# HGRN2 scan and hierarchical MoE on one core: the last two chunks routed as one, two more units halved, kept rows sent in pieces

## The chip, the cores and the metric

The kernel runs on one core of a Trainium2 chip. TensorE (PE in the profile, its weight loads PEld) multiplies; VectorE (DVE), ScalarE (ACT) and GpSimd (POOL) do element-wise work; SyncE (SP) issues most transfers, GpSimd the gathers, scatters and some small ones, ScalarE a few. The metric is the device time of one execution in microseconds (us). Before the change it is 399.38 us, the median of three runs (397.52 to 401.21).

## The reference

Inputs are q, k, v and f_logit of 4 batches x 8 heads x 768 steps x 48 (fp32), and the weights of a mixture of 4 groups x 4 experts, each 384 -> 1024 -> 384. First comes a gated linear recurrence for each head:

```python
f = 1.0 / (1.0 + np.exp(-f_logit))
for t in range(S):
    state = f[:, :, t, :, None] * state + np.einsum('bhd,bhe->bhde', k[:, :, t], v[:, :, t])
    y[:, :, t] = np.einsum('bhd,bhde->bhe', q[:, :, t], state)
```

y, with the heads side by side, gives 3072 rows x of 384 numbers. Each row goes to one expert (the best group, then the best expert of that group), and its result is scaled by both softmax weights:

```python
g_idx = np.argmax(x @ w_group, axis=1)
e_idx = np.argmax(xg @ w_expert[g], axis=1)
out[tok_idx] = combined[:, None] * (np.maximum(xg[mask_e] @ w1[g, e], 0.0) @ w2[g, e])
```

## The kernel before, in words

**Two stages.** The first stage works the recurrence off in 6 chunks of 128 steps, each in two units of two batches (`units`, NU = 12 units, numbered 0 to 11; unit i belongs to chunk i // 2). The second stage passes over the 16 experts, the fullest first ("places" 0 to 15 of a ranking), with rows gathered from a DRAM copy of x, `x_dram`. All four engines TensorE, VectorE, ScalarE and SyncE run in an order written out by hand; a wait is only for data or for a buffer.

**The written order.** For each i a list of tokens (`EVEN`, `ODD`, and `ORDERS` for i = 8 to 12) says which step of which unit comes next; `step` runs one. A token is a letter and an offset to i. `l` issues loads, `c` clamps the gate logits on VectorE, `g` makes decays on ScalarE with sums on TensorE, `m` multiplies q and k by them on VectorE, `t` transposes on TensorE, `z` copies halves of v on ScalarE, `s` makes scores (`scored`: matmuls, then a mask product on VectorE), `n` updates the states, `w` sums the outputs (`weighed`: a state part and a value part), `d` makes router logits (`done`), `x` turns the rows (`listed`), `b` transposes decays. `r` advances the routing, `e` the first two experts, `o` sends kept rows, `1` to `4` ask for the weights of the first two experts (first layers, then second layers). An engine works its own part of the list in this sequence, so what stands ahead of a step on the same engine delays it.

**Halved units.** For units in `HALVED` (3 to 8) `scored` leaves out the quarter of the score matrix that lies above the diagonal, and masks 384 instead of 512 columns; `weighed` takes 64-row pieces in the value part, and needs the v halves copied by `z`. The other units go through `scored_whole`.

**Routing.** `route` is a generator for one chunk (4 batches): best group and expert (VectorE, in two steps), ranks within the experts (`rk`, TensorE), running counts, the slots (`ln`, `head`, `val`, VectorE), the scales (written to x_dram with GpSimd, `meta`), and a table of row numbers (`tb` on TensorE, added to `table` on VectorE). With chunk 3 (CLOSE) the two fullest experts so far are named, their first 128 rows are gathered (`early`), and `fix_early` notes them in the counts; it runs inside the routing of chunk 4 as `tidy`. After the last chunk `chosen` gathers the second 128 rows of place 1 (`rows_w`), ranks all experts (`ranked`) and finds all row numbers and names (`choose`).

**Hand-over.** `early` runs under the tokens `e`: a transposing step for each of the two experts, four `up` steps each (six matmuls of 128 columns, 12 instructions, then a ReLU), and the first five of eight `down` matmuls of expert 0. Then the list ends. Next come, in program order, the transposes of the gathered second rows of place 1 (`turn_in`), the last three down matmuls, and the second half of place 1's first layer. From there on PSUM banks come from `bank` with `turns` set: it zeroes banks on VectorE as they are first taken, three with the first request, which is that of the transposes.

**Kept rows.** Rows of units 0 to 7 stay in two buffers (of the pool for second-layer weights) and go to x_dram with two transfers of 1536 KB on SyncE, at the token `o`; rows of units 8 to 11 are sent one by one by GpSimd or ScalarE (`side`).

Of the kernel before, what the change touches and what calls it, by code (L numbers as in the profile page):

```python
# [23 lines left out]
def kernel(  # L24
# [128 lines left out]
    firsts = iota([P, B * (G + 1), 4], [[0, B * (G + 1)], [-1, 4]], "firsts", base=4)  # L153
# [37 lines left out]
    limits = const([1, (ARMS - 1) * GE + 80], FP32, "limits")[:, 0:(ARMS - 1) * GE].rearrange("p (a e) -> p a e", e=GE)  # L191
# [18 lines left out]
    def route(c, lg, sb, tabled=True, tidy=None, counted=None, last=None):  # L210


        def tmp(shape, name, dtype=FP32, bufs=1):
            return sb.tile(shape, dtype, tag=name, bufs=bufs, name=name)

        SHP = (P, B * (G + 1), 4)
        L = lg.rearrange("p n (a e) -> p (n a) e", e=4)
        mx = tmp([P, B * (G + 1)], "mx")
# [4 lines left out]
        nc.vector.scalar_tensor_tensor(out=oh, in0=dl, scalar=0.0, in1=firsts, op0=OP.is_ge, op1=OP.mult)  # L223
        yield
        best = tmp([P, B * (G + 1)], "best")
        nc.vector.reduce_max(out=best, in_=oh, axis=AX)
        nc.vector.tensor_tensor(oh, oh, best.unsqueeze(2).broadcast_to(SHP), OP.is_equal)
        ohv = oh.rearrange("p (n a) e -> p n a e", n=B)
        ohe = tmp([P, B, GE], "ohe", BF16)
        nc.vector.tensor_tensor(ohe.rearrange("p n (g e) -> p n g e", e=EG), ohv[:, :, 1:G + 1, :],  # L230
                                ohv[:, :, 0, :].unsqueeze(3).broadcast_to((P, B, G, EG)), OP.mult)
        yield

        rk = bank([P, B + 1, GE], "rk")
        nc.tensor.matmul(rk[:, 0:B, :].rearrange("p n e -> p (n e)"), lhsT=strictb, rhs=ohe.rearrange("p n e -> p (n e)"), start=True, stop=False, skip_group_check=True)
        for n in range(B):
            nc.tensor.matmul(rk[:, n + 1:, :], lhsT=onesb, rhs=ohe[:, n:n + 1, :].broadcast_to((P, B - n, GE)), start=False, stop=(n == B - 1), skip_group_check=True)
        nc.scalar.activation(dl, dl, AF.Exp)
        yield
        if tidy:  # L240
            tidy(sb)
        pick = tmp([P, B, GE], "pick")
        nc.vector.tensor_tensor(pick, rk[:, 0:B, :], run.unsqueeze(1).broadcast_to((P, B, GE)), OP.add)
        nc.vector.tensor_tensor(pick, pick, ohe, OP.mult)
        nc.vector.reduce_sum(out=keys[:, c], in_=pick, axis=AX)
        nc.vector.tensor_tensor(run, run, rk[:, B, :], OP.add)
        if counted:
            counted(sb)
        yield
        ln = val = None  # L250

        def slots():

            nonlocal ln, val
            at = tmp([P, B, 2], "at", I32)
            nc.vector.tensor_copy(at[:, :, 0], keys[:, c])
            nc.vector.tensor_scalar(at[:, :, 1], at[:, :, 0], 7, None, OP.logical_shift_right)
            nc.vector.tensor_scalar(at[:, :, 0], at[:, :, 0], P - 1, None, OP.bitwise_and)
            atf = tmp([P, B, 2], "atf")
            nc.vector.tensor_copy(atf, at)  # L260
            ln = tmp([P, B, P], "ln", BF16)
            nc.vector.tensor_tensor(ln, lanes.unsqueeze(1).broadcast_to((P, B, P)), atf[:, :, 0:1].broadcast_to((P, B, P)), OP.is_equal)
            yield
            BLK = (P, B, 2 * GE)
            head = tmp(list(BLK), "head")
            nc.vector.tensor_tensor(head, heads_of.rearrange("p e j -> p (e j)").unsqueeze(1).broadcast_to(BLK), atf[:, :, 1:2].broadcast_to(BLK), OP.is_equal)
            val = tmp([P, 2, B, 2 * GE], "val", BF16)
            for m in range(2):
                nc.vector.tensor_tensor(val[:, m], head, part[:, c, :, m:m + 1].broadcast_to(BLK), OP.mult)
            yield  # L270

        def scales():

            sm = tmp([P, B, G + 1], "sm")
# [3 lines left out]
            ew = tmp([P, B, G], "ew")  # L278
            nc.vector.tensor_tensor(ew, sm[:, :, 1:G + 1], ohv[:, :, 0, :], OP.mult)
            ws = tmp([P, B], "ws")  # L280
            nc.vector.reduce_sum(out=ws, in_=ew, axis=AX)
            meta = tmp([P, B, 2], "meta", bufs=2)
            nc.vector.tensor_tensor(meta[:, :, 0], ws, sm[:, :, 0], OP.mult)
            nc.gpsimd.tensor_copy(meta[:, :, 1].bitcast(I32), token[:, c, :])
            nc.gpsimd.dma_start(out=rows_of(c)[:, :, DM:RW], in_=meta)
            yield

        for part_of in (scales, slots) if last else (slots, scales):
            if tabled or part_of is scales:
                yield from part_of()  # L290
        if tabled:
            tb = bank([P, 2, GE, 2], "tb")
            for b in range(B):
                nc.tensor.matmul(tb.rearrange("p m e j -> p m (e j)"), lhsT=ln[:, b], rhs=val[:, :, b, :], start=(b == 0), stop=(b == B - 1))
# [191 lines left out]

    def room(w, shape, name):

        own_size = {"bufs": 1} if w["pool"] is ep and name == "h" else {}
        full = w["pool"].tile([P, shape, P if w["pool"] is ep else WIDE], FP32, tag=name, name=name, **own_size)  # L490
        w[name[:2].replace("xe", "xT") + "_full"] = full
        return full[:, :, 0:w["n"]]
# [116 lines left out]
    def early():  # L609
# [6 lines left out]
        full = ep.tile([P, FO, WIDE], FP32, tag="h_full", bufs=1, name="h_full")  # L616
        ws[WHOLE].update(h=full[:, :, 0:P], h_full=full)
        nc.gpsimd.tensor_copy(told, ws[0]["x"][:, 0, DM:RW])
# [9 lines left out]
    with ExitStack() as fast:  # L628
# [36 lines left out]
        HALVED = range(3, NU - 3)  # L665
# [166 lines left out]
        def weighed(i):  # L832
# [13 lines left out]
            for asked in (E, L) if i in HALVED else ():  # L846
                for a in range(HP):
# [11 lines left out]
        def done(i):  # L859
# [3 lines left out]
            if s == 0:  # L863
                groups[c] = sb.tile([P, B, NL], FP32, tag="lgs", name="lgs")
            lT = bank([P, P], "lT")
            for a in range(HP):
                for b in range(2):
                    at = 32 * (2 * b + a % 2)
                    nc.tensor.matmul(lT[at:at + 32, :], lhsT=gw[:, b, a, :], rhs=xT[:, b, a, :], start=(a < 2), stop=(a >= 2), skip_group_check=True, tile_position=(0, at))
# [5 lines left out]
            nc.vector.reduce_sum(out=groups[c][:, 2 * s:2 * s + 2, :], in_=lg[:, :, :, 0:NL].rearrange("p b j l -> p b l j"), axis=AX)  # L875
            if s:
                routes.append(routed(c))
# [43 lines left out]
        def routed(c):  # L921

            yield from route(c, groups[c], sb, tidy=fix_early if c == CLOSE + 1 else None, counted=load_early if c == CLOSE else None,
                             last=chosen if c == NC - 1 else None)
# [13 lines left out]
        def advance(gens):  # L938
# [24 lines left out]
        def step(nm, i):  # L963
# [6 lines left out]
            elif nm == "o":  # L970
                send_kept(i - (NU - 4))
# [266 lines left out]
```

## Time and profile before

| what | us |
|---|---|
| median of three runs | 399.38 |
| lowest and highest | 397.52, 401.21 |
| the profiled execution | 398.24 |
| its span, first to last instruction | 396.4 |
| TensorE busy in the span | 388.4 (98%) |
| VectorE busy | 285.8 (72%) |
| ScalarE busy | 164.4 (41%) |
| GpSimd busy | 90.3 (23%) |

Matmuls are pipelined and their ends are modelled, so the busy time of TensorE tells where it had work and not how fast it did it. A chain of waits goes back from the last instruction to what released each step; a run of TensorE pieces in it means that nothing else held the kernel there. The granted clock of TensorE is 0.997 of full speed (2.4 GHz) over the span.

### The profile page before, as it was taken

What the parts mean: (1) busy time and instruction counts of PE and PEld (TensorE: products, weight loads), DVE (VectorE), ACT (ScalarE), POOL (GpSimd) and SP (SyncE); (2) the same over time, 40 slices, a digit from 0 to 9 for tenths busy, and PEclk for the clock granted to TensorE, in tenths of its full rate; (3) what the DMA queues carried; (4) which work ended last, traced back from release to release, by engine and by line L of the source; (5) the groups of instructions that cost most, each with busy time, mean ns of one, the idle gap of its engine ahead of it and who ended that gap; (6) DMA issues with size and microseconds to landing.
All of it is one profiled execution on the core that took longest, in us unless ns stands there. A gap on an engine that the chain in (4) does not pass through costs nothing.

```text
span 396.4 us, 10685 instructions
## 1 busy us (share of the span) xinstructions
PE 388.4 (98%) x4150; PEld 361.7 (91%) x4150; DVE 285.8 (72%) x845; ACT 164.4 (41%) x368; POOL 90.3 (23%) x171
## 2 busy tenths in 40 slices
PE   8999999999999999999999999999999999999994
PEld 3888888888888979999999999999999999999992
DVE  6766788878998687970999949578687585596530
ACT  6777888888665311222312223123131232232130
POOL 7000010101031157102042222321320430110241
PEclk9999999999999999999999999999999999999998
DMA  9999989799969849994938659578587596585110
GB/s 188 216 200 204 199 169 183 145 186 258 258 207 382 310 145 330 387 389 187 318 100 316 212 193 347 157 279 267 175 330 236 180 361 201 194 333 170 34 50 28
DMA packets 133038, 89.44 MB, mean 226 GB/s; under 512 B 103441, under 2 KB 123619, under 8 KB 132955
## 3 DMA queue, kind: packets, MB, share of 16 engines
q1 hardware_dynamic: 125666, 75.50, 63.8%
q0 software_dynamic: 6656, 11.93, 9.5%
q8 instruction: 62, 1.02, 1.0%
q10 hardware_dynamic: 632, 0.83, 0.6%
q14 instruction: 22, 0.17, 0.1%
HBM read 78.71 MB, written 9.89 MB: 223 GB/s over the span
## 4 chain that ended last, share of the span: by engine, by line
PE 73%; issue 15%; DMA 4%; POOL 3%; DVE 2%; POOLq 1%; ACT 1%; ACTq 0%
PE held L534 20%; PE held L579 19%; PE cs L717 4%; DMA out_dram<-yt,xg 3%; PE x_ps L894 3%; PE ap L803 3%; PE y L845 3%; PE y L853 3%; POOL out_dram L553 3%; PE tr_q L749 3%; PE tr_k L749 2%; PE hp L534 2%; PE y L841 2%; PE ap L788 2%; PE ds L821 2%
## 5 line engine op out<-in xcount | busy, mean ns | idle before, releaser
L534 PE MATMUL held<-xe,w 128*128 128x128 f32 (+13 forms) x768 | 122.3, 319 | 0.4 <-issue 0.4
L534 PEld LDWEIGHTS held<-xe,w 128*128 128x128 f32 x768 | 120.0, 190 | 1.3 <-issue 1.0
L514 DVE STREAM_TRANSPOSE yr<-yT 32x192 f32<-32x192 f32 (+1 forms) x224 | 76.8, 343 | 53.2 <-ACT yT L580 50.1
L579 PE MATMUL held<-h,w 128*128 128x192 f32 (+12 forms) x672 | 110.8, 325 | 0.0
L579 PEld LDWEIGHTS held<-h,w 128*128 128x128 f32 x672 | 109.0, 190 | 0.0
L507 DVE STREAM_TRANSPOSE xe<-xg 32x192 f32<-32x192 f32 (+1 forms) x240 | 80.3, 335 | 5.1 <-DMA xg<-x_dram,rows_p 1.6
L535 ACT ACTIVATE h<-held 128x478 f32<-128x478 f32 (+14 forms) x60 | 30.1, 502 | 86.9 <-PE held L534 86.9
L553 POOL DMA_INDIRECT out_dram<-yt,xg x31 | 35.6, 1148 | 131.4 <-ACT yt L550 124.9
L580 ACT COPY yT<-held 128x256 f32<-128x256 f32 (+14 forms) x45 | 14.7, 331 | 80.3 <-PE held L579 77.7
L484 POOL DMA_INDIRECT xg<-x_dram,rows_p x29 | 29.1, 1005 | 53.9 <-DMA out_dram<-yt,xg 28.2
L722 POOL DMA_DIRECT2D ends<-eq x10 | 5.4, 545 | 77.4 <-ACT eq L718 66.7
L806 DVE TENSOR_TENSOR am<-ap,tri 128x512 f32<-128x512 f32 x24 | 15.1, 690 | 7.5 <-PE ap L803 7.5
L550 ACT ACTIVATE yt<-yr,xg 128x384 f32<-128x384 f32 (+13 forms) x28 | 15.5, 604 | 7.2 <-DVE yr L514 7.2
L717 PE MATMUL cs<-ld_f,tri 128*128 128x384 f32 x48 | 18.2, 498 | 0.2 <-ACT ld_f L711 0.2
L856 ACT COPY xT<-y 128x512 f32<-128x512 f32 x24 | 13.4, 587 | 5.5 <-PE y L845 4.3
L749 PE MATMUL tr_q<-ident,qh 128*128 128x128 f32 x96 | 14.5, 273 | 0.5 <-issue 0.5
L750 ACT COPY Tk<-tr_k 128x512 f32<-128x512 f32 x24 | 14.6, 615 | 0.0
L750 ACT COPY Tq<-tr_q 128x512 f32<-128x512 f32 x24 | 14.4, 601 | 0.4 <-PE tr_q L749 0.3
L791 DVE TENSOR_TENSOR am<-ap,seen 128x384 f32<-128x384 f32 x24 | 12.2, 551 | 3.2 <-PE ap L788 3.2
L749 PE MATMUL tr_k<-ident,kh 128*128 128x128 f32 x96 | 14.3, 273 | 0.0
L718 ACT ACTIVATE eq<-cs 128x384 f32<-128x384 f32 x24 | 12.6, 525 | 3.8 <-PE cs L717 3.8
L894 PE MATMUL x_ps<-ident,xT 128*128 128x128 f32 x96 | 13.4, 279 | 0.0
(216 smaller groups left out, 475.9 us busy)
## 6 DMA issues: line engine op xcount, KB each, us to landing
w<-in_moe_w_dram SPq DMA_DIRECT2D x34, 1536.0 KB, 12.9
qh<-in_q_dram SPq DMA_DIRECT2D x12, 384.0 KB, 5.6
ld_k<-in_k_dram SPq DMA_DIRECT2D x12, 384.0 KB, 5.4
v<-in_v_dram SPq DMA_DIRECT2D x12, 384.0 KB, 6.2
ld_f<-in_f_logit_dram SPq DMA_DIRECT2D x11, 384.0 KB, 6.6
x_dram<-x_kept SPq DMA_DIRECT2D x2, 1536.0 KB
x_dram<-x POOLq DMA_DIRECT2D x2, 384.0 KB, 5.7
x_dram<-x ACTq DMA_DIRECT2D x2, 384.0 KB
```

Source lines behind the costliest of these rows:

```text
L484: nc.gpsimd.indirect_dma_start(out=w["x"][:, j, :], out_offset=None, in_=x_dram[0:1 + top, :], in_offset=bass.IndirectOffsetOnAxis(ap=rows ...
L507: squares(w, lambda n, k_, rk, g, rg: nc.vector.transpose(out=xT[rg, 0:n, k_], in_=x[rk, 0:n, g]))
L514: squares(w, lambda n, k_, rk, g, rg: nc.vector.transpose(out=y[rk, 0:n, g], in_=yT[rg, 0:n, k_]))
L534: nc.tensor.matmul(hp[:, o, 0:m], lhsT=w1[:, ko, (f + o) * P:(f + o + 1) * P], rhs=w["xT"][:, ko, 0:m], start=(ko == 0), stop=(ko == KO - 1))
L535: nc.scalar.activation(h[:, f:f + 2, :], hp, AF.Relu)
L550: nc.scalar.activation(y[0:m], yp[0:m], AF.Copy, scale=scale)
L553: sent = nc.gpsimd.indirect_dma_start(out=out, out_offset=bass.IndirectOffsetOnAxis(ap=token_of.bitcast(U32), axis=0), in_=y[0:m], in_offs ...
L579: nc.tensor.matmul(yp[:, 0:c], lhsT=w2[:, fo, m * P:(m + 1) * P], rhs=w["h"][:, fo, 0:c], start=(fo == 0), stop=(fo == FO - 1))
L717: nc.tensor.matmul(cs.rearrange("t h d -> t (h d)"), lhsT=tri, rhs=nl[:, b], start=True, stop=True)
L749: nc.tensor.transpose(out=pt[:, a, :], in_=w[nm + "h"][:, b, 2 * a:2 * a + 2, :].rearrange("t r d -> t (r d)"), identity=ident)
L750: nc.scalar.copy(w["T" + nm][:, b], pt)
L894: nc.tensor.transpose(out=pt[:, a].rearrange("t h d -> t (h d)"), in_=xT[:, b, a, :], identity=ident)
```

## The change

- `route` takes n chunks. Chunks 4 and 5 go through it as one, with 8 batches to an operation (`NB`), after the last logits; their scales are one write. Their buffers are twice as large for all.
- `fix_early` is a token of its own, `f`, at the end of the list of i = 10.
- `HALVED` goes to unit 10; in units 9 and 10 the value part takes its groups of heads in the sequence 2, 3, 0, 1. The lists have `z` there.
- The token `o` is gone. `send_kept` sends one unit's rows (384 KB) at a time, behind each load of units 10 and 11.
- The lists of i = 8 to 12 are rewritten: `r` leaves i = 11, `c+2` moves up and `n-1` back in i = 9, `e` and `r` of i = 12 are dealt out anew.
- The h buffer of the first early expert is the second half of `h_full`.

```diff
-        HALVED = range(3, NU - 3)
+        HALVED = range(3, NU - 1)
...
-        rk = bank([P, B + 1, GE], "rk")
-        nc.tensor.matmul(rk[:, 0:B, :]..., lhsT=strictb, rhs=ohe...)
-        for n in range(B):
-            nc.tensor.matmul(rk[:, n + 1:, :], lhsT=onesb, rhs=ohe[:, n:n + 1, :].broadcast_to((P, B - n, GE)), ...)
+        rk = bank([P, NB + 1, GE], "rk")
+        nc.tensor.matmul(rk[:, 0:NB, :]..., lhsT=strictb, rhs=ohe...)
+        for m in range(NB):
+            nc.tensor.matmul(rk[:, m + 1:, :], lhsT=onesb, rhs=ohe[:, m:m + 1, :].broadcast_to((P, NB - m, GE)), ...)
...
-            nc.gpsimd.dma_start(out=rows_of(c)[:, :, DM:RW], in_=meta)
+            nc.gpsimd.dma_start(out=rows_of(c, 0, NB)[:, :, DM:RW], in_=meta)
...
-                for a in range(HP):
+                for a in range(HP) if i < NU - 3 else (2, 3, 0, 1):
...
+        ws[0]["h"] = full[:, :, P:WIDE]
...
-            if s:
-                routes.append(routed(c))
+            if s and c == at + n - 1:
+                routes.append(routed(at, n))
...
-        def send_kept(j):
-            nc.sync.dma_start(out=rows_of(2 * j, 0, 2 * B)[:, :, 0:DM], in_=rows_kept[j])
+        def send_kept(i, count=1):
+            while i >= NU - 2 and count and len(kept_sent) < 4 * (i - NU + 3):
+                j = len(kept_sent)
+                kept_sent.append(j)
+                c, s = units[j]
+                nc.sync.dma_start(out=rows_of(c, 2 * s, 2)[:, :, 0:DM], in_=rows_kept[j // 4][:, j % 4 * 2:j % 4 * 2 + 2, :])
+                count -= 1
...
-            NU - 4: "l+2 o d-2 n-1 r r r t t t t g+1 g+1 z s s w s s d-1 x-1 x-1 x-1 r c+2 g+2 w g+2 n m+1 m+1".split(),
-            NU - 3: "l+2 o d-2 r r t t t t r g+1 g+1 r b n-1 s s s s c+2 w d-1 x-1 x-1 x-1 g+2 w g+2 n m+1 m+1 r n".split(),
-            NU - 2: "d-2 r x-1 x-1 r t t t t g+1 g+1 r 1 x-1 s s s s w d-1 w n m+1 m+1 2 3".split(),
-            NU - 1: "d-2 r r n-1 x-1 x-1 t t t t r x-1 r s s s s 4 w b d-1 w r r".split(),
-            NU: "d-2 r e d-1 x-1 x-1 d-1 x-1 r r r e e r e r r e r r e e r e r r e e e".split(),
+            NU - 4: "l+2 d-2 n-1 r r r t t t t g+1 g+1 z s s w s s d-1 x-1 x-1 x-1 r c+2 g+2 w g+2 n m+1 m+1".split(),
+            NU - 3: "l+2 d-2 r r c+2 t t t t r g+1 g+1 r b z s s w s s d-1 n-1 x-1 x-1 x-1 g+2 w g+2 n m+1 m+1 r n".split(),
+            NU - 2: "d-2 x-1 t t t t g+1 g+1 r r r z 1 s s w s s d-1 x-1 x-1 w 2 m+1 m+1 f 3".split(),
+            NU - 1: "d-2 t t t t x-1 x-1 x-1 s s s s 4 w b d-1 w".split(),
+            NU: "d-2 e d-1 x-1 x-1 d-1 x-1 r r e e e r e r r e r r e e e r r r e e".split(),
...
-                    load(i, ("k", "qh"))
+                    load(i, ("k",))
+                    send_kept(i)
+                    load(i, ("qh",))
+                    send_kept(i)
                     if i + 1 < NU:
                         load(i + 1, ("f",))
+                        send_kept(i)
                     load(i, ("v",))
+                    send_kept(i, 4)
```

## Rows read from the trace of the kernel before

**Rows 1.** Windows, two stretches: length, then busy us of each engine (instructions), clock, DMA, GB/s.
```profile
97.33:108.50 11.17, 10.95 (x180) 9.24 (x179) 9.95 (x29) 7.81 (x19) 0.74 (x1) 1.00 1.02 269
108.50:118.40 9.90, 9.90 (x150) 8.55 (x147) 9.33 (x30) 6.16 (x15) 3.13 (x4) 1.00 0.65 206
```

**Rows 2.** Chain of waits, unit 8 (halved): start us, us, piece.
```profile
90.91 0.83 PE ap L788 x32
91.73 0.88 PE y L841 x32
92.61 0.67 PE ap L788 x32
...
94.99 1.62 PE y L853 x64
```

**Rows 3.** Chain of waits, unit 9 (whole).
```profile
101.36 1.99 PE ap L803 x32
103.34 1.03 PE y L841 x32
...
105.98 1.90 PE y L845 x32
```

**Rows 4.** Chain of waits, last logits to the end of expert 0's down matmuls.
```profile
129.68 0.12 PE lg L874
...
131.75 0.20 PE rk L235
...
132.04 5.46 PE hp L534 x48
137.50 0.12 PE tb L294 x4
137.61 4.10 PE hp L534 x36
141.71 3.23 PE yo L563 x10
144.94 0.33 PE held L521 x3
145.27 1.94 PE yo L563 x6
```

**Rows 5.** Timeline of VectorE, last route and hand-over: start us, us, what [idle before].
```profile
130.37 0.24 DVE L221 TENSOR_TENSOR dl<-lgs,mx 128x80 f32<-128x80 f32 x1
...
134.96 0.69 DVE L262 TENSOR_TENSOR ln<-lanes,atf 128x512 bf16<-128x512 f32 x1
...
137.65 0.22 DVE L297 TENSOR_TENSOR table<-table,tb 128x64 f32<-128x64 f32 x1 [1.27 <-PE tb L294]
...
143.46 1.56 DVE L91 MEMSET held<- 128x512 f32 x3
145.30 0.56 DVE L522 COPY xe<-held 128x384 f32<-128x384 f32 x1 [0.28 <-PE held L521]
```

**Rows 6.** Timeline of GpSimd: the last scale write and the gather of place 1.
```profile
134.77 0.79 POOL L285 DMA_DIRECT2D x_dram<-meta  x1 [4.22 <-issue]
139.93 1.02 POOL L484 DMA_INDIRECT xg<-x_dram,rows_w  x1 [4.37 <-DVE less L324]
```

**Rows 7.** DMA issues, 80 to 165 us: count, KB each, median us to landing.
```profile
ld_f<-in_f_logit_dram SPq DMA_DIRECT2D x2, 384.0 KB, 7.0
...
x_dram<-x POOLq DMA_DIRECT2D x2, 384.0 KB, 5.7
...
x_dram<-meta POOLq DMA_DIRECT2D x4, 4.0 KB, 4.4
...
xg<-x_dram,rows_w POOLq DMA_INDIRECT x1, 3.2
```

**Rows 8.** Timeline of SyncE: the gate load of unit 11.
```profile
90.03 1.00 SPq L692 DMA_DIRECT2D ld_f<-in_f_logit_dram  x1
```

**Rows 9.** Mask products on VectorE by shape, 80 to 125 us: count, busy us, mean ns.
```profile
L806 DVE TENSOR_TENSOR am<-ap,tri 128x512 f32<-128x512 f32 x12 | 7.6, 697 | 0.3 <-PE ap L803 0.3
L791 DVE TENSOR_TENSOR am<-ap,seen 128x384 f32<-128x384 f32 x8 | 4.0, 551 | 1.2 <-PE ap L788 1.2
```

More of the change, by code (lines that the diff above doesn't have):

```diff
@@ L208, in restart, with route @@
         nc.vector.tensor_copy(run, base)
-    def route(c, lg, sb, tabled=True, tidy=None, counted=None, last=None):
+    def route(c, lg, sb, n=1, tabled=True, counted=None, last=None):
+        NB = n * B
+        cs = slice(c, c + n)
         def tmp(shape, name, dtype=FP32, bufs=1):
-            return sb.tile(shape, dtype, tag=name, bufs=bufs, name=name)
-        SHP = (P, B * (G + 1), 4)
+            size = math.prod(shape[1:])
+            t = sb.tile([P, size * 2 // n], dtype, tag=name, bufs=bufs, name=name)[:, 0:size]
+            dims = "abcd"[0:len(shape) - 1]
+            return t.rearrange(f"p ({' '.join(dims)}) -> p {' '.join(dims)}", **dict(zip(dims, shape[1:])))
+        SHP = (P, NB * (G + 1), 4)
         L = lg.rearrange("p n (a e) -> p (n a) e", e=4)
-        mx = tmp([P, B * (G + 1)], "mx")
+        mx = tmp([P, NB * (G + 1)], "mx")
         nc.vector.reduce_max(out=mx, in_=L, axis=AX)
@@ L222, in route @@
         oh = tmp(list(SHP), "oh")
-        nc.vector.scalar_tensor_tensor(out=oh, in0=dl, scalar=0.0, in1=firsts, op0=OP.is_ge, op1=OP.mult)
+        nc.vector.scalar_tensor_tensor(out=oh, in0=dl, scalar=0.0, in1=firsts[:, 0:NB * (G + 1)], op0=OP.is_ge, op1=OP.mult)
         yield
-        best = tmp([P, B * (G + 1)], "best")
+        best = tmp([P, NB * (G + 1)], "best")
         nc.vector.reduce_max(out=best, in_=oh, axis=AX)
         nc.vector.tensor_tensor(oh, oh, best.unsqueeze(2).broadcast_to(SHP), OP.is_equal)
-        ohv = oh.rearrange("p (n a) e -> p n a e", n=B)
@@ L238, in route @@
+        for m in range(NB):
+            nc.tensor.matmul(rk[:, m + 1:, :], lhsT=onesb, rhs=ohe[:, m:m + 1, :].broadcast_to((P, NB - m, GE)), start=False, stop=(m == NB - 1), skip_group_check=True)
         nc.scalar.activation(dl, dl, AF.Exp)
         yield
[L240 to L243, printed above, removed]
+        key = keys[:, cs].rearrange("p c b -> p (c b)")
@@ L244, in route @@
+        pick = tmp([P, NB, GE], "pick")
+        nc.vector.tensor_tensor(pick, rk[:, 0:NB, :], run.unsqueeze(1).broadcast_to((P, NB, GE)), OP.add)
         nc.vector.tensor_tensor(pick, pick, ohe, OP.mult)
-        nc.vector.reduce_sum(out=keys[:, c], in_=pick, axis=AX)
-        nc.vector.tensor_tensor(run, run, rk[:, B, :], OP.add)
+        nc.vector.reduce_sum(out=key, in_=pick, axis=AX)
+        nc.vector.tensor_tensor(run, run, rk[:, NB, :], OP.add)
         if counted:
@@ L292, in route @@
             tb = bank([P, 2, GE, 2], "tb")
-            for b in range(B):
-                nc.tensor.matmul(tb.rearrange("p m e j -> p m (e j)"), lhsT=ln[:, b], rhs=val[:, :, b, :], start=(b == 0), stop=(b == B - 1))
+            for b in range(NB):
+                nc.tensor.matmul(tb.rearrange("p m e j -> p m (e j)"), lhsT=ln[:, b], rhs=val[:, :, b, :], start=(b == 0), stop=(b == NB - 1))
             if last:
@@ L485, in fetch, with whole_h @@
         return w
+    def whole_h():
+        return ep.tile([P, FO, WIDE], FP32, tag="h_full", bufs=1, name="h_full")
     def room(w, shape, name):
-        own_size = {"bufs": 1} if w["pool"] is ep and name == "h" else {}
-        full = w["pool"].tile([P, shape, P if w["pool"] is ep else WIDE], FP32, tag=name, name=name, **own_size)
+        if w["pool"] is ep and name == "h":
+            return whole_h()[:, :, 0:w["n"]]
+        full = w["pool"].tile([P, shape, P if w["pool"] is ep else WIDE], FP32, tag=name, name=name)
         w[name[:2].replace("xe", "xT") + "_full"] = full
@@ L615, in early @@
             yield
-        full = ep.tile([P, FO, WIDE], FP32, tag="h_full", bufs=1, name="h_full")
+        full = whole_h()
         ws[WHOLE].update(h=full[:, :, 0:P], h_full=full)
+        ws[0]["h"] = full[:, :, P:WIDE]
         nc.gpsimd.tensor_copy(told, ws[0]["x"][:, 0, DM:RW])
@@ L862, in done @@
             xT = live[i]["xT"]
-            if s == 0:
-                groups[c] = sb.tile([P, B, NL], FP32, tag="lgs", name="lgs")
+            at = c // 2 * 2 if c > CLOSE else c
+            n = 2 if c > CLOSE else 1
+            if s == 0 and c == at:
+                groups[c] = sb.tile([P, n * B, NL], FP32, tag=f"lgs{n}", bufs=3 - n, name="lgs")
+            lgs = groups[at][:, (c - at) * B + 2 * s:(c - at) * B + 2 * s + 2, :]
             lT = bank([P, P], "lT")
@@ L867, in done @@
                 for b in range(2):
-                    at = 32 * (2 * b + a % 2)
-                    nc.tensor.matmul(lT[at:at + 32, :], lhsT=gw[:, b, a, :], rhs=xT[:, b, a, :], start=(a < 2), stop=(a >= 2), skip_group_check=True, tile_position=(0, at))
+                    to = 32 * (2 * b + a % 2)
+                    nc.tensor.matmul(lT[to:to + 32, :], lhsT=gw[:, b, a, :], rhs=xT[:, b, a, :], start=(a < 2), stop=(a >= 2), skip_group_check=True, tile_position=(0, to))
             lgT = sb.tile([P, P], FP32, tag="lgT", name="lgT")
@@ L919, in load_next, with routed @@
             weights.setdefault(p, []).append(load_layer(wp, value(who_late[0:1, layer - 1, p:p + 1], GE - 1), layer))
-        def routed(c):
-            yield from route(c, groups[c], sb, tidy=fix_early if c == CLOSE + 1 else None, counted=load_early if c == CLOSE else None,
-                             last=chosen if c == NC - 1 else None)
+        def routed(c, n):
+            yield from route(c, groups[c], sb, n, counted=load_early if c == CLOSE else None, last=chosen if c > CLOSE else None)
             if c == CLOSE:
@@ L969, in step @@
                 next(pad)
-            elif nm == "o":
-                send_kept(i - (NU - 4))
+            elif nm == "f":
+                fix_early(sb)
             elif nm in "1234":
```

42 lines of the change are left out of this document (22 added, 20 removed).

## The prediction

> **What bounds the kernel now.** I read the windows of the changed stage first, then the chain of waits, then VectorE's and GpSimd's timelines, last the DMA landings. In the two stretches in which units 9 and 10 are worked off, TensorE is busy 10.95 of 11.17 us and 9.90 of 9.90, at a granted clock of 1.00; VectorE comes second with 9.95 and 9.33 [rows 1]. From the last logits to the first matmul of place 1's second half the chain is TensorE alone, piece after piece [rows 4]. So time is won by taking work from TensorE and lost by making it wait. What comes after 147.2 us (the rest of the sixteen experts, TensorE filled) moves with that point: the next expert's weights are asked for when TensorE frees their buffer. I sum up to that point and carry the difference to the end.
>
> **Halving units 9 and 10.** A whole unit spends 1.99 + 1.03 + 1.90 = 4.92 us on scores, state part and value part [rows 3]; a halved one 0.83 + 0.88 + 0.67 + 1.62 = 4.00 [rows 2]. Saved: 0.92 a unit, 1.84 for two. The state part (1.03 against 0.88) is the same 32 matmuls, so the low end leaves it out: 0.77 a unit, 1.54. Two ScalarE copies of v halves a unit are added; ScalarE is busy 7.81 of 11.17 and 6.16 of 9.90 us [rows 1], so they lie beside TensorE. Value matmuls of these units take masks of heads 2 and 3 of a quartet first, so TensorE needs the last masks earlier; that is in rival C.
>
> **One route for chunks 4 and 5.** On TensorE the rank matmuls go from two sets of 224 columns to one of 704, the table matmuls stay eight. A table set of 256 columns takes 0.12 us [rows 4], so the ranks cost 0.33 where two sets cost 0.21 and the last one began behind a short wait; chunk 4's set leaves the stretch before the last logits (0.1 won), the rest evens out. Taken: 0.1 won.
>
> What matters is where the table stands. Call T the end of the last logits, 129.80 [rows 4]. Before, five of the eight up steps of the early experts stood ahead of the last table, at T + 7.7, and 4.10 (three steps) + 3.23 (the first ten down matmuls) = 7.33 us of TensorE work stood between it and the transposes of the gathered second block of place 1 [rows 4]. In the new order seven up steps stand ahead, table at T + 7.7 + 2 x 1.37 = T + 10.4, and 1.37 + 3.23 = 4.60 us behind. Behind the table VectorE runs a fixed chain: table add 0.03 us after the matmuls, place 1's rows, the ranking of all experts, their names, then the zeroing of the banks of the next stage, three at 0.52 us [rows 5]. The transposes write the first of these banks, so they need its zeroing, done at 143.46 + 0.52 = 143.98: 6.36 us behind the table's end at 137.62. Before, 7.33 covered that, with 0.97 to spare. Now 4.60 doesn't: **TensorE waits 1.76 us**. The bounds: if the transposes wait for the gather alone, it starts 2.31 us behind the table [rows 6] and lands 3.2 later [rows 7], 5.5 in all: a wait of 0.9; at the low end nothing, if neither is awaited where I think. Afterwards place 1's copy (two more zeroings and 0.56 [rows 5]) ends 7.96 behind the table, the six remaining matmuls at 6.36 + 0.33 + 1.94 = 8.63: covered.
>
> Is VectorE ready for the table by T + 10.4? An operation grows from 0.24 us for 80 elements to 0.69 for 512 [rows 5], 1.04 ns an element. Lane comparison began at T + 5.2; now ranks come about 1.2 later (two up steps ahead instead of one, less the wait) and nine doubled operations ahead of it add 0.8: T + 7.2. It takes 0.69 + 0.53, heads and values about 1.1: T + 9.5. Covered by 0.9. The scale write, one of 8 KB instead of two of 4, starts at T + 5.0 + 2.0 = T + 7.0 [rows 6]. The gather reads what it writes; at the median landing of 4.4 [rows 7] that is T + 11.4, before place 1's rows at about T + 12. Its bounds are rival D.
>
> **Pieces.** Both sends of kept rows (1.5 MB) become eight of 384 KB between unit 10's and 11's loads, on SP's queue. Unit 11's gate load, issued at 90.03 [rows 8], with a median landing of 7.0 [rows 7] there at 97.0, now stands behind two pieces. How long a piece holds the queue no row shows: at most a 384 KB row write's full 5.7 us [rows 7], at least nothing, since the same bytes went before. By the stage's 269 GB/s [rows 1] two pieces are 2.9 us: 99.9. Its clamp is moved up in VectorE's order, behind the logits that open the first stretch (97.6) and seven short operations (0.24 us and a gap each [rows 5]): needed at 99.5. It is 0.4 late; behind it wait chunk 3's rank sums, then the ranking, then unit 9's masks, which have most of that to spare. I take 0.1 lost; the ends are 0 and 108.4 - 99.5 = 8.9 us. The other loads have an order's time in hand. The rule of the Trainium skill, DMA: Bandwidth & Descriptors, section Bandwidth, speaks against this part: transfers should be at least 1 MiB. By its fixed 2.0 us a DMA and 436 GB/s (section Anatomy of one DMA) two pieces would hold the queue an estimated 5.8 us, the clamp would be 3.3 us late and the time 402.5; no row here shows it.
>
> **At no cost.** The four early weight loads are asked for by the same steps of the chunk-3 route as before: same place, no gain. The early ranking fix (five operations, 1 us on VectorE) moves ahead of the third of them; that one is only read by the down matmuls, ten us after the first up. The state update of unit 8 moves behind masks, needed an order later. The h half shared by expert 0 and place 1's second block is written only after the matmuls that read it; were the two halves held apart badly, a 0.4 us wait would fall into the 1.76.
>
> **Sum.** -1.84 - 0.1 + 1.76 + 0.1 = -0.1 us. Against the profiled execution's own 398.24 (span 396.4 and 1.8 around it) that is 398.1; the runs' median stands 1.14 higher, so **399.3 us**: no change. The halving's gain is given back at the hand-over.
>
> **Rivals.**
>
> B: the hand-over waits less than I say. For it: the zeroed bank is never read before it is overwritten, and the gather alone would cost 0.9. Against: the transposes write where VectorE has just written, so an order must be kept. Time: 397.5 (no wait) to 398.4.
>
> C: VectorE, second with 9.95 of 11.17 and 9.33 of 9.90 us, becomes the bound of orders 9 and 10. The masks fall from 697 to 551 ns [rows 9], four a unit: 0.58, so two units win 1.17 instead of 1.84: 400.0. Against: part of its time was slack behind TensorE. The Trainium skill, TensorEngine Tiling (Array Packing), section PSUM Bottleneck, says that tiling speeds up TensorE and not the reading of PSUM. By that rule the sum is 400.0, by the TensorE rows 399.3.
>
> D, **slower**: the scale write lands late and holds the gather. For it: the landing of these writes has no one size (median 4.4 [rows 7]). Against: the queues are nearly empty by then. If 8 KB takes twice the 4.4, it lands at T + 15.8, the gather starts 0.9 later and lands at T + 19.9, where the zeroing was done at T + 17: 2.9 us more, 402.2. It decides from a landing of 5.8 us on (T + 12.8, from where the gather outlasts the zeroing).
>
> E, slower: each piece holds the queue for its whole 5.7 us, unit 11's gate load is 8.9 late and unit 9's masks with it: 408. Against: the load before it and the one behind it share the engines, and the stage's bytes don't grow.
>
> **Chances.** A (forecast) 0.46, B 0.25, C 0.12, D 0.07, E 0.04, something unnamed 0.06. A measurement of this kernel tells 1%, 4.0 us, from no change: the bounds are 395.4 and 403.4. A and C stay inside; of B a tenth falls below by the runs' scatter of 1.9 either way, with half of the unnamed 0.06; of D a quarter, most of E and some of the unnamed lie above: 0.07. The rest, 0.87, is within 1%. Range: B's lower end less half the scatter, 396.6, to C and D's lower part, 401.6.
>
> **What would show it.** TensorE idle of about 1.8 us ahead of the place-1 transposes, released by VectorE's zeroing; the table 10.4 us behind the last logits; units 9 and 10 with scores of 1.5 us; VectorE's clamp of unit 11 waiting under 1 us; the gather starting 2.3 us behind the table. Wrong if the idle time isn't there (B), if masks hold the value matmuls (C), if the gather is released by the scale write (D), or if the clamp waits several us (E).

## The result and the profile after

The change makes the kernel slower. The median after is 403.1 us (402.48 to 405.67, six runs), that of the kernel before 399.07 (six runs); the ratio is 1.0104, 95% interval 1.0077 to 1.0132. The forecast was 399.3 with a range to 401.6, so both the size and the answer "no change" were wrong. The profiled execution took 402.48 us, its span is 400.7, 4.2 longer than before.

The windows of the two stretches that answer to [rows 1], and two of 3 us inside the first (length; busy us of PE, PEld, DVE, ACT, POOL with instructions; granted clock; DMA share; GB/s), kernel after:

```profile
97.18:110.87 13.69, 11.98 (x247) 9.85 (x244) 10.87 (x34) 8.63 (x21) 0.93 (x2) 0.88 1.02 251
110.87:119.90 9.03, 9.03 (x214) 7.77 (x210) 7.75 (x26) 6.80 (x16) 2.41 (x3) 1.00 0.46 130
103.00:106.00 3.00, 1.51 (x48) 1.10 (x40) 1.30 (x4) 0.90 (x2) 0.00 (x0) 0.94 0.99 226
106.00:109.00 3.00, 3.00 (x47) 2.46 (x40) 2.90 (x5) 1.56 (x5) 0.00 (x0) 0.50 1.05 248
```

The second stretch is shorter than before (9.03 for 9.90), as the halving should make it. The first is longer (13.69 for 11.17), with 1.7 us in which TensorE does nothing and a stretch at the lower clock level (0.50 is 1.2 GHz). The chain of waits shows both (start us, us, piece), kernel after:

```profile
102.97 0.32 PE ap L798 x13
103.29 1.49 issue
104.78 0.66 PE ap L798 x14
...
106.25 1.90 PE x_ps L907 x8
108.15 2.07 PE y L863 x64
...
114.79 0.83 PE ap L798 x32
115.62 0.88 PE y L851 x32
116.49 0.67 PE ap L798 x32
...
118.32 1.65 PE y L863 x64
...
130.94 0.11 PE lg L887
...
141.18 0.25 PE tb L299 x8
...
147.26 0.50 DVE held L91
...
147.80 0.33 PE held L530
```

Unit 10 is done in 0.83 + 0.88 + 0.67 + 1.65 = 4.03 us, a halved unit's price [rows 2, 3]. In unit 9 TensorE stands 1.49 us from 103.29 on, in the middle of a row of equal matmuls that wait for nothing that the profile shows, and its work up to 109 runs in the main at half clock. The table ends at 141.43, and the transposes of the hand-over begin at 147.80, 6.37 behind it: the forecast was 6.36. TensorE's waits in this stretch (engine, line, what it waited for: us, times, longest), kernel after:

```profile
PE held L530 <- DVE held L91: 1.7, 1, 1.7
PE ap L798 <- issue: 1.5, 1, 1.5
```

GpSimd's timeline, first of the kernel before, then of the kernel after (start us, us, what, idle time before it and what ended it):

```profile
110.59 0.71 POOL L902 DMA_DIRECT2D x_dram<-x  x1 [3.01 <-ACT x L899]
...
113.82 0.76 POOL L285 DMA_DIRECT2D x_dram<-meta  x1 [2.31 <-issue]
116.95 2.65 POOL L484 DMA_INDIRECT xg<-x_dram,rows_e  x1 [2.37 <-DVE am L806]
```

```profile
114.90 0.77 POOL L290 DMA_DIRECT2D x_dram<-meta  x1 [4.94 <-DVE meta L288]
117.95 1.07 POOL L489 DMA_INDIRECT xg<-x_dram,rows_e  x1 [2.29 <-DVE am L801]
...
124.23 0.19 POOL L628 COPY told<-xg 128x2 f32<-128x2 f32 x1 [3.33 <-DMA xg<-x_dram,rows_e]
124.47 0.77 POOL L915 DMA_DIRECT2D x_dram<-x  x1
```

The row send of unit 9 left at 110.59, ahead of chunk 3's scale write and the early gathers. Now it leaves at 124.47, behind both gathers and behind the copy of `told`, which has to wait until a gather has landed. The prediction's paragraph on moved steps doesn't name it. What it releases is the buffer `x` (two of them): unit 11's copy on ScalarE waits 2.7 us for it here, and up to 5.4 in the runs below.

Of TensorE's way, in three traces of the first kind of chip (starts of instructions; the five stretches sum to the span but for rounding):

| stretch, us | before | after | a_again (the same kernel) |
|---|---|---|---|
| start to unit 7's logits | 97.27 | 97.18 | 97.85 |
| to unit 11's logits | 32.25 | 33.59 | 30.86 |
| to the table's end | 8.10 | 10.64 | 13.11 |
| to the transposes of the hand-over | 7.16 | 6.38 | 6.38 |
| to the end | 251.67 | 252.87 | 252.14 |

In the first trace the 4.2 us are made up of 1.34 in the order of the units (1.84 were to be won there), 1.76 up to the transposes of the hand-over (as forecast) and 1.20 behind them, where the prediction took everything to move along unchanged.

### The profile page after: what moved, and what is told of

It is laid out like the page before. It is cut to its first block, busy times and chain, and to the rows that moved or that the text cites. A ratio compares the mean times of both kernels' runs of the same rounds, so it can differ in the third digit from the quotient of the medians.

```text
span 400.7 us, 10925 instructions
## 1 busy us (share of the span) xinstructions
PE 388.6 (97%) x4277; PEld 361.5 (90%) x4277; DVE 282.1 (70%) x820; ACT 165.9 (41%) x371; POOL 88.1 (22%) x169
## 4 chain that ended last, share of the span: by engine, by line
PE 43%; issue 28%; DMA 11%; DVE 8%; POOL 7%; POOLq 1%; ACT 1%; DVEq 0%
DMA out_dram<-yt,xg 10%; PE held L543 6%; PE held L588 4%; PE cs L727 4%; PE y L863 3%; POOL out_dram L562 3%; PE x_ps L907 3%; PE ap L798 3%; DVE xe L516 3%; POOL xg L489 2%; PE tr_k L759 2%; PE hp L543 2%; PE tr_q L759 2%; PE y L851 2%; PE ds L831 2%
## 5 line engine op out<-in xcount | busy, mean ns | idle before, releaser
L801 DVE TENSOR_TENSOR am<-ap,seen 128x384 f32<-128x384 f32 x32 | 16.2, 550 | 5.2 <-PE ap L798 5.2
L798 PEld LDWEIGHTS ap<-Tq,Tk 48*64 48x64 f32 x512 | 13.1, 133 | 5.3 <-issue 2.0
L816 DVE TENSOR_TENSOR am<-ap,tri 128x512 f32<-128x512 f32 x16 | 9.9, 684 | 10.0 <-PE ap L813 10.0
L798 PE MATMUL ap<-Tq,Tk 48*64 48x128 f32 (+1 forms) x512 | 14.6, 247 | 1.5 <-issue 1.5
```

The costliest lines, as they stand in the source:

```text
L798: nc.tensor.matmul(ap[r][to, j, at, :], lhsT=w["Tk"][rows, b, 2 * m + j, keys], rhs=w["Tq"][rows, b, 2 * m + j, asked], start=True, stop=True)
L801: nc.vector.tensor_tensor(am[:, r].rearrange("p a n t -> p a (n t)"), ap[r].rearrange("p a n t -> p a (n t)"), mask, OP.mult)
```

## The experiments

The runs fell on chips of two kinds. On the first, the kernel before takes 399.1 us; on the second 407.5 to 408.5, with one further stop that b_third traces. So times are compared on one chip only, as ratios to the kernel before there.

**The same kernels again (first kind of chip).** No edit.

> The changed kernel again, unedited, for its time and a second trace beside the others. All theories: 1.01 of the kernel before. If the stop for code is a matter of chance in each execution (as two of four traces of halved variants suggest), its place and length differ from the first trace (1.49 us in unit 9's scores).

> The kernel before, unedited, for a trace beside the others on the same chip. All theories: no stop in units 8 to 11 above 0.3 us; the last table ends 8 us behind the last logits, 137 to 138 us.

The kernel before: span 395.9. The changed kernel: 402.37 us, ratio 1.0078 (1.0053 to 1.0104). The loss is real, but it is made up otherwise. TensorE stands only 0.41 us in the order of the units, and their stretch is 1.4 us shorter (forecast: 1.84). The table is late instead. TensorE's waits, then ScalarE's longest, of a_again:

```profile
PE hp L543 <- ACT x L909: 1.8, 1, 1.8
PE held L530 <- DVE held L91: 1.7, 1, 1.7
PE ds L831 <- issue: 0.4, 1, 0.4
PE tb L299 <- DVE val L274: 0.4, 1, 0.4
```

```profile
ACT x L909 <- DMA x_dram<-x: 5.4, 1, 5.4
```

And its chain of waits up to the table:

```profile
125.76 7.70 DMA x_dram<-x
...
133.54 0.09 ACT x L909
...
135.40 0.56 ACT h_full L544 x2
135.96 0.23 ACT dl L244
...
136.21 0.33 DVE sm L280
...
140.59 0.77 DVE val L274 x2
...
141.41 0.42 PE tb L299 x8
```

Read from below: the table waits for VectorE's values, these for the scales that VectorE works out first, these for ScalarE's Exp, and that stands on ScalarE behind unit 11's copy, which waits for unit 9's rows to land. In this execution the transfer that the change put behind the early gathers sets the end of the table.

**Pieces, halving, bank (second kind of chip).** e1_big_sends sends the kept rows in two transfers again; e2_whole works units 9 and 10 whole; e3_plain_bank takes the transposes of the hand-over out of the zeroed bank; e4_big_plain is e1 and e3 together.

```diff
# e1
-   nc.sync.dma_start(out=rows_of(c, 2 * s, 2)..., in_=rows_kept[j // 4][...])    (eight, between loads)
+   nc.sync.dma_start(out=rows_of(2 * j, 0, 2 * B)..., in_=rows_kept[j])          (two, at o of units 8 and 9)
# e2
-   HALVED = range(3, NU - 1)
+   HALVED = range(3, NU - 3)
# e3
-   turns.append(1)
    turn_in(ws[0])
+   turns.append(1)
```

> The changed kernel, with the kept rows sent as before: two transfers of 1536 KB behind the loads of units 10 and 11. In the changed kernel TensorE stops for 1.49 us in unit 9's scores, and then runs at half clock for some 3 us, 1.56 us more. Theory 1 (the small pieces keep the queues full just when TensorE's next 16 KB of code is due, and it runs dry): the code packet comes by about 100.7, no stop, no half clock, 3 us faster than the changed kernel, 400.0 us. Theory 2 (halving unit 9 uses up code faster than it can come, pieces or not): the stop stays, 403 us.

> The changed kernel, with units 9 and 10 whole again, pieces kept. Theory 1: the code packet is as late as in the changed kernel (about 102), the stop and the half clock stay at least in part, and the halving's 1.84 us are lost on top: 404 to 405 us. Theory 2: fewer instructions per us in unit 9, no stop, 3.05 us won and 1.84 lost: 401.9 us.

> The changed kernel, with the transposes of the gathered second rows of place 1 written to an ordinary bank, so that they need no zeroing; the zeroed banks begin with the matmuls behind them. In the changed kernel TensorE waits 1.77 us there, until 6.37 us behind the table. If the zeroing is the cause (as predicted), the gather is next, 1.9 + 3.2 us behind the table: TensorE waits 0.5 us, 1.2 us faster than the changed kernel, 401.9 us. If the gather is the cause, the wait stays at 1.8 and the time at 403.1.

> Both edits: big sends as before and the ordinary bank for the transposes. By theory 1 and the zeroing together: 403.1 - 3.05 - 1.2 = 398.8 us, about as the kernel before. By theory 2: 401.9 us.

Ratios 1.0091 (1.0058 to 1.0124), 1.0094 (1.0079 to 1.0109), 1.0091 (1.0072 to 1.0109) and 1.0065 (1.0047 to 1.0083). The changed kernel itself was not run on this chip; elsewhere it has 1.0078 to 1.0107. e1 still has TensorE's stops (1.06 and 0.44 us), so the pieces don't cause them. e2 has none, and is no faster: what the halving won, the stops took. Its stretch from unit 7's to unit 11's logits takes 32.45 us where the kernel before has 32.25, so the new orders by themselves cost some 0.2. The bank did in the trace what was expected. TensorE's wait at the hand-over in e3:

```profile
PE xg_ps L530 <- DMA xg<-x_dram,rows_w: 0.6, 1, 0.6
```

The wait falls from 1.74 to 0.61 and the gather ends it: VectorE's zeroing was what TensorE waited for. In e3's time the 1.1 us less don't show. e4 differs from e1 in the bank alone and its median is 1.2 us lower (411.06 for 412.24), but the two intervals overlap. So the worth of the bank in the time stays open. Against 399.07 us the expected times are ratios of 1.002 or 1.010 for e1, 0.999 or 1.007 for e4, 1.012 to 1.015 or 1.007 for e2, and 1.007 or 1.010 for e3: e1 and e4 lie at their second theories, e2 and e3 between the two.

**Halving alone, and sends spread out (first kind).** f1_halved_only is the kernel before with units 9 and 10 halved, with the sequence 2, 3, 0, 1 that goes with it, and nothing else. e5_spread is the changed kernel with the kept pieces dealt out behind the loads of units 5 to 11, two and then one each.

```diff
# f1, on the kernel before
-   HALVED = range(3, NU - 3)
+   HALVED = range(3, NU - 1)
-   ... n-1 s s s s c+2 w ...     ... x-1 s s s s w ...
+   ... n-1 z s s w s s c+2 ...   ... x-1 z s s w s s ...
# e5
-   while i >= NU - 2 and count and len(kept_sent) < 4 * (i - NU + 3):
+   while i >= BEGUN + 2 and count and len(kept_sent) < i - 3:
```

> The kernel before with units 9 and 10 halved and nothing else: routes, kept rows and hand-over as before. If halved units use code faster than it comes through full queues (theory 2), TensorE stops for 0.3 to 1.5 us in units 9 or 10, and of the 1.84 us that halving takes away little is left: between -1.5 and +1.2 us against the kernel before. If the pieces are the cause (theory 1): no stop, 1.8 us faster than the kernel before.

> The changed kernel with each unit's kept rows sent two units after it, one piece of 384 KB behind the loads of each of units 5 to 11, instead of eight pieces behind those of units 10 and 11. If full queues delay the code (theory 1, or 2 with contention), the code packets of units 9 and 10 come in time, no stop and no half clock, up to 3 us faster than the changed kernel. If the rate of halved units alone is too high, the stop stays.

f1: 398.6 us, ratio 0.9995 (0.9969 to 1.002): the halving alone wins nothing that can be measured, and 0.2 us up to the last logits in the trace (32.02 for 32.25). Its waits, behind ScalarE's xT and VectorE's masks, say why in part; in the order written for whole units the masks come too late:

```profile
PE x_ps L894 <- ACT xT L856: 0.3, 1, 0.3
...
PE y L853 <- DVE am L791: 0.2, 1, 0.2
```

All waits of this stretch that the kernel before doesn't have make 0.6 us of the 1.6 that are missing; the rest isn't placed.

e5: 402.54 us, 1.0075 (1.0046 to 1.0104): as the changed kernel. It has the wait behind ScalarE's x (1.65 us) with three pieces in the place of eight behind 85 us, so that wait isn't the pieces' doing either. Its trace has no stop between unit 7's and unit 11's logits, but 0.59 and 0.38 us at 56.7 and 67.6, where pieces now go. One execution doesn't show that stops follow the pieces, and e1's stops speak against it.

**Unit 9's send by another queue, and the mendings together (second kind).** g1_other_queue issues it from ScalarE; g3_and_start adds e3's bank and moves the larger fill of `firsts` behind the other constants; g4_all_big adds e1's sends. Each was run on two chips (g1b, g3b and g4b are the same kernels), the second time with the kernel before traced beside them (b_third, no edit).

```diff
# g1
-   side(i).dma_start(out=rows_of(c, 2 * s, 2)[:, :, 0:DM], in_=x...)
+   (nc.scalar if i == NU - 3 else side(i)).dma_start(out=rows_of(c, 2 * s, 2)[:, :, 0:DM], in_=x...)
# g3, beside e3's edit
    nc.gpsimd.memset(blank, 0.0)
+   nc.gpsimd.iota(firsts, pattern=[[0, 2 * B * (G + 1)], [-1, 4]], ...)      (from ahead of base)
```

> The changed kernel with unit 9's row send issued by ScalarE instead of GpSimd, two buffers of x as they were. Theory (moved send): the send leaves some 10 us earlier (about 114 instead of 124 to 126) because nothing of the route is ahead of it; it has landed by 122, unit 11's copy waits for nothing, and the time is that of the kernel with three buffers, ratio 1.003-1.006. Rival (the transfer itself, not the queue, is late, since other transfers fill the DMA engines): it still lands behind 130 and the waits stay, ratio 1.008-1.010.

> The changed kernel with three things mended at once: unit 9's send from ScalarE, the held transposes kept out of the zeroed bank (the stop of 1.74 us fell to 0.6 when that was tried alone), and the larger fill of firsts put behind the other constants of the start. Theory (the three costs add): against the changed kernel -2 for the send, -1.1 for the bank and -0.3 for the start, together about -3.4 of 402.4: 399.0, ratio 0.998-1.002. Rival (one of the three hides another): no better than 400.6, ratio 1.004 or more.

> The kernel with the three mendings and, beside them, the kept rows sent again in two pieces of 1536 KB from the lists of units 8 and 9, as before. If the eight pieces cost nothing (the two sizes gave 1.0091 each when only that was undone), the time is that of the three mendings alone, ratio 0.998-1.002, within 0.3% of it. Rival (the pieces fill the DMA engines when the early rows and unit 9's rows have to go, which the other waits hid so far): 0.3 to 0.6% faster than the three mendings alone, ratio 0.993-0.997, and so faster than the kernel before.

> The kernel before, unedited, for its trace on the chip of the three runs below. If this chip is the one on which the kernels took 408 to 412 us: theory (that chip adds a wait of its own behind the hand-over): the kernel before has the stop in place 1's second layer as well (L588 behind ACT h_full, 6 to 10 us), its next expert starts 24.8 us behind the table like the others', and its span is 405 to 407. Rival (only the changed kernels have it): no such stop. If it is the first chip: span 395.9 to 396.4, no stop.

> Unit 9's send from ScalarE once more, the rest as changed. On the first chip, theory (moved send): ACT x L909 <- DMA x_dram<-x and PE hp L543 <- ACT x L909 are gone, the table ends 10.3 to 10.7 us behind the last logits, the ratio is 1.003-1.006 where the changed kernel has 1.008-1.010. Rival (the wait only takes the place of another): ratio 1.008-1.010. On the second chip 1.0054 as measured there.

> The three mendings (send, bank, start) once more. On the first chip, theory (the costs add): -2.0, -1.1 and -0.3 us from the changed kernel's 402.4: 399.0, ratio 0.998-1.002. Rival (a stop of TensorE for its code in units 9 and 10, which falls differently in every kernel and execution, takes what is gained): ratio 1.003 or more with gaps at L798 or L863 of over 1 us. On the second chip 1.0049 as measured there, where the stop in place 1 swallows what is gained ahead of it.

> The three mendings with the kept rows in two pieces once more. Theory (the pieces cost nothing): within 0.2% of the three mendings alone, ratio 0.998-1.002. Rival: 0.3% or more below them, and below the kernel before.

g1: 1.0054 (1.003 to 1.0078) and 1.0026 (1.0007 to 1.0044): the loss is about halved (the changed kernel, not run on these two chips, has 1.0078 to 1.0107 on three others), the table ends 10.64 us behind unit 11's logits in both traces, and ScalarE's wait is gone. A third buffer for `x`, which would have parted the wait from the queue, does not fit (g0_three_tiles: 59 KB a partition are needed, 57.4 are left), so that way stays untested. The other mendings, expected to bring the time back to that of the kernel before, don't add to it: g3 has 1.0049 (1.003 to 1.0068) and 1.0036 (1.0012 to 1.0059), g4 1.0047 (1.0027 to 1.0068) and 1.0039 (1.0014 to 1.0063). So no version beat the kernel before. g3 and g4 differ in the size of the sends alone and their ratios agree to 0.03%, with intervals of 0.2% either way. The start isn't shown as a cause: unit 0's logits begin at 26.93 to 27.35 us with the fill moved and at 27.02 to 27.44 without.

b_third settles the further stop: the kernel before has it too. Windows of the kernel before on the first kind of chip, then of b_third (columns as above), and b_third's wait:

```profile
153.00:161.00 8.00, 8.00 (x44) 8.00 (x43) 7.67 (x21) 0.74 (x2) 5.49 (x6) 1.00 1.02 341
```

```profile
153.00:161.00 8.00, 0.60 (x4) 0.25 (x2) 7.68 (x21) 0.39 (x1) 4.87 (x6) 0.71 1.04 360
161.00:166.00 5.00, 5.00 (x14) 4.57 (x15) 2.26 (x7) 0.76 (x2) 0.00 (x0) 0.50 1.04 395
```

```profile
PE held L579 <- issue: 7.4, 1, 7.4
```

It belongs to these chips, not to the change.

**That one step alone, and undone (second kind, one chip).** k1_moved_alone is the kernel before with only the last two steps of unit 9's rows (the transposes and copies of its second half, and the send) at the end of unit 10's order; k2_moved_back is the changed kernel with them back at its head; a_third is the changed kernel, unedited.

```diff
# k1, on the kernel before
-   "d-2 r x-1 x-1 r t t t t g+1 g+1 r 1 x-1 s s s s w d-1 w n m+1 m+1 2 3"
+   "d-2 r x-1 r t t t t g+1 g+1 r 1 s s s s w d-1 x-1 x-1 w n m+1 m+1 2 3"
# k2, on the changed kernel
-   "d-2 x-1 t t t t g+1 g+1 r r r z 1 s s w s s d-1 x-1 x-1 w 2 m+1 m+1 f 3"
+   "d-2 x-1 x-1 x-1 t t t t g+1 g+1 r r r z 1 s s w s s d-1 w 2 m+1 m+1 f 3"
```

> The kernel before with one part of the change alone: the second and third step of unit 9's row send moved to where the changed kernel has them, at the end of the list of unit 10, which puts the send behind the scale write, the two early gathers and the copy of told on GpSimd's queue. Theory (moved send): unit 9's send leaves at 125 to 126 instead of 110.6, lands at 131 to 133, and unit 11's copy into the same buffer (129.3 before) waits for it 2 to 4 us; the stages behind it on ScalarE and TensorE start 1.5 to 2 us later, so the table ends 1.5 to 2 us later and the ratio to the kernel before is 1.003-1.005. Rival (it needs the merged route to hurt, since the kernel before has other work to fill the wait): the wait is on ScalarE alone, the table does not move, ratio 0.999-1.001.

> The changed kernel with the same two steps moved back to the head of the list of unit 10, so that unit 9's send is ahead of the scale write again. Theory (moved send): the send leaves at 111 to 113, no wait of ScalarE for x_dram<-x, the table ends 10.3 to 10.7 us behind the last logits, and the kernel is 0.4 to 0.5% faster than the changed kernel of the same call. Rival (the other costs take the place of the wait): less than 0.2% faster.

> The changed kernel, unedited, on the chip of these runs: the measure for the kernel with the two steps moved back. Theory and rival alike: ratio to the kernel before 1.008-1.010, as on the other two chips, with either a wait of TensorE behind ScalarE's copy of x (1.7 us) or a stop for code in units 9 and 10 ahead of it.

k1: 410.18 us against 407.99, ratio 1.0052 (1.0033 to 1.0071). k2: 410.37, 1.004 (1.0021 to 1.0059). a_third: 413.36, 1.0107 (1.0082 to 1.0133). Doing the step costs 2.2 us and undoing it gives 3.0 of the 5.4 that the change costs there. GpSimd and ScalarE in k1, with the send behind `told` and the wait for it:

```profile
125.40 0.19 POOL L618 COPY told<-xg 128x2 f32<-128x2 f32 x1 [4.06 <-DMA xg<-x_dram,rows_e]
125.64 0.77 POOL L902 DMA_DIRECT2D x_dram<-x  x1
```

```profile
ACT x L896 <- DMA x_dram<-x: 3.0, 1, 3.0
```

What reaches TensorE of it, in k1:

```profile
PE hp L534 <- ACT x L896: 0.4, 1, 0.4
```

Of TensorE's waits, the two behind the send in a_third, then the longest two of k2:

```profile
PE hp L543 <- ACT x L909: 1.2, 1, 1.2
...
PE tb L299 <- DVE val L274: 0.4, 1, 0.4
```

```profile
PE held L530 <- DVE held L91: 1.8, 1, 1.8
PE xg_ps L530 <- DMA xg<-x_dram,rows_e: 0.5, 1, 0.5
```

With the step back the two waits behind ScalarE's x and VectorE's values are gone, and the table ends 10.64 us behind unit 11's logits where a_third has 12.51. k2 gains more than the 0.4 to 0.5% expected of it. One thing doesn't fit: k1's own trace has the table only 0.6 us later than before (8.71 behind the logits for 8.10), less than the 1.5 to 2 expected and than the 2.2 measured. Its span is 2.6 us longer than b_third's (another chip of this kind): 1.0 of it stands ahead of unit 7's logits, before the moved step can act, 0.15 up to unit 11's logits, 0.6 up to the table, and 0.85 behind the hand-over. So of the cost that k1 measures, the trace puts 0.6 us down to the wait; the cause of the rest is open.

## Why the prediction was wrong

**The step that failed first: "At no cost".** It lists the moved steps and leaves out unit 9's row send. It was moved, so that on GpSimd a scale write, two gathers and a copy that waits for a gather now stand ahead of it, and its buffer is wanted by unit 11. Rows that could have shown it were in the trace of before: the send, the gathers and `told` on one timeline. ScalarE's wait for it is in all eight traces of versions that leave the send there (2.7 to 5.4 us). The cost: 1.9 to 2.5 us of table delay in the three of them with the longest waits, 4.8 to 5.4 us, which reach TensorE (12.51, 12.99 in e5 and 13.11, where most others have 10.64 and none over 11.4), and by the times 2.2 us in k1 and 3.0 in k2. None of the rivals was this one.

**The halving's term, -1.84, was mis-sized.** A unit's price was right (4.03 for 4.00). What was missed is that TensorE stops without any wait that the profile shows, and with units 9 and 10 halved it does so there in most executions. Up to unit 11's logits, 14 executions with the changed orders and halved units: six have at most 0.41 us of such stops and win 0.97 to 1.49 against before (mean 1.28); eight have 0.9 to 1.9 us and lose 0.43 on average, the first trace the most but one, with 1.49 of stop and, behind it, 1.53 more for x_ps, lT and y at the lower clock than unit 10 and the like pay (1.90, 0.80 and 2.07 for 1.02, 0.57 and 1.65). Over all 14 this stretch wins 0.3 us, not 1.84. The 0.56 by which even the six fall short of 1.84 is in part the short stops that some of them have and in part the 0.2 that the new orders cost in e2. The five executions with whole units there (the kernel before three times, k1 and e2) have no such stop. f1, the 15th with halved units, wins 0.2 and waits for masks: rival C named that, and it holds in the old order only. The Trainium skill, TensorEngine Tiling (Array Packing), section PSUM Bottleneck, cited for that rival, says tiling doesn't speed up reading PSUM; f1's waits agree, with 0.2 us for the masks and 0.3 for ScalarE.

**The two losses stand in for each other.** In the execution first profiled the stop made unit 11 so late that the send had almost landed: ScalarE waited 2.7 us and TensorE not at all. In a_again there was only the short stop, and the wait came. Both took 402 us, with nearly the same table end (141.4 and 141.8). That is why the first trace alone pointed at the stop. It isn't one or the other in every execution: e2 and e4, with no stop and 0.27 us of it, have the table only 0.7 and 0.3 us late.

**The hand-over was right.** Forecast 1.76, measured 1.74; the transposes 6.36 behind the table's end, measured 6.37; the table's matmuls beginning at T + 10.4, measured 141.18 - 131.05 = 10.1 where nothing held them. The lower bound, 0.9 if the gather alone counts, answers to e3's 0.6. Rival B falls with it.

**Pieces, D and E.** The pieces cost nothing that the times can tell (g3 against g4). Unit 11's gate load was issued at 91.74 on SyncE, behind two pieces that held the queue 1.94 and 1.74 us, 3.68 us together where the prediction had 2.9 by the stage's rate and 5.8 by its other estimate, and the clamp of unit 11 did not wait for it:

```profile
91.74 0.41 SPq L702 DMA_DIRECT2D ld_f<-in_f_logit_dram  x1
```

The Trainium skill, DMA: Bandwidth & Descriptors, section Bandwidth, would have transfers of 1 MiB or more; here eight of 384 KB and two of 1536 KB give the same time (ratios 1.0049 and 1.0047, 1.0036 and 1.0039). D: the last gather began 1.9 us behind the table, released by VectorE and not by the scale write, which had landed at 142.19:

```profile
138.16 0.94 POOL L290 DMA_DIRECT2D x_dram<-meta  x1 [12.93 <-issue]
143.34 1.02 POOL L489 DMA_INDIRECT xg<-x_dram,rows_w  x1 [4.23 <-DVE rkey L327]
```

**What is open.** After the send is put back, 0.3 to 0.5% is left (g1, k2). The forecast's own sum for that kernel was zero; with the 0.3 us of the 14 executions in place of 1.84 it would be 1.5 us, 0.4%. That agrees, but no run took the stops away, and the sum leaves out another step that failed: "I sum up to that point and carry the difference to the end". Behind the hand-over's transposes the first kind of chip has 251.7 and 251.9 us in the kernel before, and 252.1 to 252.9 in after, a_again and e5; the second kind has 261.5 in b_third, and 261.8 to 263.7 in the versions that keep the zeroed bank. The traced executions of g1 and k2 have 0.28 us of stops and none, and are still 1.8 and 1.9 us longer than b_third. What costs time behind the hand-over is not shown.

## What to carry to other kernels

Write out each queue's order before and after, engine by engine, DMAs too, and for every transfer that has changed its neighbours ask which buffer it frees and who wants it next; a copy that waits for a gather holds back every transfer that the same engine issues behind it. Look at a second execution before believing the first trace's largest gap, because two losses can cover each other. A saving in matmul time that comes with more and shorter instructions should be checked for stops that no semaphore explains.

## What the runs showed of the hardware

TensorE's stops go with the arrival of its code. The trace has transfers of the kind instruction; those of 16 KB stand on a queue of their own, 62 in each kernel with whole units 9 and 10 and 63 in each with halved ones, which have 256 to 258 more matmuls and weight loads. The row of that queue (kind: packets, MB, share), kernel after, from 100 to 104 us:

```profile
q8 instruction: 1, 0.02, 1.9%
```

That packet of 16 KB began at 102.22 and ended at 103.41; the stop lasts from 103.29 to 104.78, so TensorE went on 1.37 us behind it. The packet ahead of it had begun at 94.20, 8.0 us earlier; in a_again the two before its stop are 5.8 us apart and the stop is 0.41. In g3, where the distance is 8.2, the stop is again 1.49, but the granted clock stays at 1.00 behind it. In the 14 executions with the changed orders and halved units there are 16 stops between unit 7's and unit 11's logits; 13 end 1.2 to 1.5 us behind the end of such a packet, the other three (0.40 to 0.45 us) 4.5 to 4.8. The distance alone doesn't decide: in the traces of the kernel before packets are up to 9.3 us apart there without a stop. Why a packet comes later in one execution than in the next is open, and that the late packet is the cause is read from these times; no run moved it.

In every trace of the second kind of chip ScalarE's ReLU of place 1's second half comes late and TensorE stops 7 to 10 us in all, then runs 7 to 14 us at half clock, whatever the kernel. What ScalarE waits for isn't in the records.
